# Copies of k and v between partitions in three uneven pieces, ranked setup operations and a new table of places, in a two-layer attention and mixing kernel

## The chip, the cores and the metric

The kernel runs on one core of one Trainium2 chip. The metric is the device time of one execution in microseconds. TensorE is called PE below, VectorE DVE, ScalarE ACT, GpSimd POOL, and SyncE SP. SP only issues DMAs here; ACT issues a few too.

## The reference

Two layers with the same weights, each made of two blocks, on x of 2048 positions by 512 features (fp32):

```python
x = x + A(layernorm(x));  x = x + B(layernorm(x))      # twice
# A: q, k, v = x @ wqkv, 32 heads of 16; position s looks at s, s-2, ..., s-14 (8 positions, dilation 2),
#    positions before 0 masked with -1e9; softmax over the 8; o @ wo
# B: h = gelu(layernorm(x) @ w1); its four quarters of 128 features shifted by +1, -1, +2, -2 positions; @ w2;
#    x1 = x + that;  x1 + gelu(layernorm(x1) @ w3) @ w4     (w3 is 512 x 1792)
```

## The kernel before

The 2048 positions are worked on in four blocks of 512, twice (two layers), so there are eight steps n = 0 to 7. Within a block, tile i (0 to 3) holds 128 positions: partitions 0 to 63 hold even positions and 64 to 127 odd ones ("parity"), and partition p of tile i stands for position 8p + 2i (+1) of the block. In this layout the window of dilation 2 runs along the free axis: k and v stand in buffers `kv` of 11 slots of 128 numbers, 7 of pad (the positions before) and 4 of the block's own. The pad slots of a partition are the own slots of the partition above it: slots 3 to 6 come from one partition above, slots 0 to 2 from two partitions above. There are three `kv` buffers.

For block 0 the kernel takes a short way (`p1_quarters`): q, k and v are computed in fp32 for a quarter of the heads at a time (qt 0 to 3), and the shifted pad slots are made by DMA copies between partitions of SBUF (in `p2_unit`, n = 0). Quarter 0 is written straight to `kv` buffers, quarters 1 to 3 to `x` buffers first. The copies of quarter 0 for parity 1 are issued by ACT, all others by SP. The other blocks (`p1_stream`) split fp32 numbers into two fp16 parts (tiles named `_hl`, three products for one), store q, k and v to DRAM (`q_d`, `kv_d`) through three buffers `ev`, and load the windows from there.

The attention itself (`p2_unit`) is on DVE: products of k with q over the window, sums, softmax (the exponential on ACT), products with v, a tree of sums to `o`. For each n there are four such units, one for each quarter of the heads. `p3` transposes and splits `o` to `oT` (`turn_pe`, `split`), multiplies by wo and goes on to w1; `p4` does the shifted product with w2; `p5` the MLP.

Nothing is issued in the order in which it is written. Every operation is an `Op` with a list of engines and expected durations; `Graph` finds what depends on what, and `plan` simulates the engines: at each point of simulated time, a free engine takes the ready operation with the lowest key among those for which buffers are free. The key of the k-th operation made is `PLACES[k]`, a table of ranks. What `plan` returns is issued, engine by engine, in that order; on the chip each engine works in order and waits on semaphores.

```python
o.key, o.alts, o.succ, o.n, o.est = PLACES[len(self.ops)], alts, [], 0, 0.0
...
for e in (PE, ACT, DVE, POOL, SP):
    if free[e] > now or not ready[e]:
        continue
    ...
        it = heapq.heappop(ready[e])
```

Before the first ranked operation stand setup instructions in written order: 64 warm-up products on PE, memsets of the mask, of the pad slots and of zeros, and a store of zeros to the head of `kv_d` of layer 2, issued by ACT. All ranked operations are issued through one helper, so that the profile shows them all with its line, L363; the tiles' names tell them apart.

Of the kernel before, what the change touches and what calls it, by code (L numbers as in the profile page):

```python
# [199 lines left out]


class Op:
    __slots__ = ("key", "alts", "succ", "n", "est", "touch", "seq", "fn", "end", "xfer", "eng", "lend")


class Graph:
# [3 lines left out]
    def __call__(self, key, alts, r=(), w=(), after=(), xfer=0.0):  # L210
# [34 lines left out]
        return o  # L245


LAT, LAT_PE, LAT_SP, LAT_DMA, TABLE = 0.12, 0.4, 0.3, 2.3, 1.3


def plan(ops, slots):
# [97 lines left out]
def tile_mixer(ctx, tc, x_d, wqkv_d, wo_d, w1_d, w2_d, w3_d, w4_d, out_d):  # L349
# [599 lines left out]
    def p2_unit(n, qt):  # L949
# [76 lines left out]
        for i in (0, 2):  # L1026
# [25 lines left out]
            if n == 0 and i and qt == 3:  # L1052
                o_.lend = LENT
# [316 lines left out]
```

## Time and profile before

| | |
|---|---|
| time, median of 3 runs | 1227.99 us (1225.02 to 1229.84) |
| profiled execution | 1225.26 us, of which the span of its instructions 1223.5 us |
| PE busy | 1188.0 us (97%) |
| DVE busy | 930.2 us (76%) |
| ACT busy | 629.3 us (51%) |
| POOL busy | 386.4 us (32%) |
| mean granted clock of PE | 0.992 |
| moved by DMA | 176.73 MB |

A row of a timeline has the start, the time, the engine (PEld is PE's weight load; SPq and ACTq are queues in which a DMA is issued), the line, the operation, the tiles as out<-in without buffer numbers, the shapes and how many; in brackets the idle time before and what ended it. A row of waits has who waited for whom, the microseconds in total, the times, and the longest one. A row of a table of stretches has the busy time of each engine, the granted clock of PE (1.00 is full speed), the DMA engines' mean share and GB/s.

### The profile page before, as it was taken

How to read it: one execution, taken by the hardware profiler on the slowest of the kernel's cores; microseconds unless marked ns; L12 is line 12 of the kernel's file. 1: busy time of each engine (PE TensorE's matmuls, PEld its weight loads, DVE VectorE, ACT ScalarE, POOL GpSimd, SP SyncE). 2: the span in 40 equal slices, each digit the busy share in tenths (PEclk: the TensorE clock that was granted, in tenths of full speed). 3: DMA queues.
4: the chain of work that ended last, by engine and by line, in shares of the span. 5: the costliest groups of instructions: out<-in, count | busy, mean ns of one | idle time of the engine just before them, and what ended most of it. 6: DMA issues, size and time to landing. Idle time of an engine off the chain costs nothing.

```text
span 1223.5 us, 15971 instructions
## 1 busy us (share of the span) xinstructions
PE 1188.0 (97%) x5676; PEld 589.8 (48%) x5676; DVE 930.2 (76%) x1082; ACT 629.3 (51%) x1102; POOL 386.4 (32%) x534
## 2 busy tenths in 40 slices
PE   9887889999999999999999999999999999999998
PEld 7433444555444454544454444444454444445544
DVE  4588988998889989999984899798974999414212
ACT  4543476534875345655464446555653556444422
POOL 6311265302541234314451325212632372211000
PEclk9989999999999999999999999999999999999999
DMA  5656575885676665564436543685147434111322
GB/s 172 183 161 174 148 192 168 241 233 151 191 225 173 167 169 123 132 178 116 122 90 174 159 110 110 175 201 134 59 138 214 135 91 146 61 62 48 108 77 69
DMA packets 129599, 176.73 MB, mean 144 GB/s; under 512 B 11504, under 2 KB 72912, under 8 KB 129520
## 3 DMA queue, kind: packets, MB, share of 16 engines
q1 hardware_dynamic: 127216, 173.78, 51.0%
q10 hardware_dynamic: 2304, 1.95, 0.6%
q8 instruction: 44, 0.72, 0.3%
q14 instruction: 35, 0.29, 0.1%
HBM read 132.64 MB, written 37.87 MB: 139 GB/s over the span
## 4 chain that ended last, share of the span: by engine, by line
PE 71%; DMA 0%; DVE 0%; ACT 0%; issue 0%
PE mm L363 50%; PE acc L363 21%; DMA w<-w 0%; DVE x L363 0%; ACT ev L363 0%
## 5 line engine op out<-in xcount | busy, mean ns | idle before, releaser
L363 PE MATMUL acc<-w,g 128*128 128x512 f16 (+1 forms) x1260 | 307.4, 393 | 0.2 <-DMA w<-in_B_w_dram 0.2
L363 PE MATMUL mm<-nT,w 128*128 128x512 f16 (+1 forms) x1288 | 301.5, 388 | 0.7 <-ACT nT L363 0.7
L363 PE MATMUL mm<-wq_hl,xt 128*128 128x512 f16 x1008 | 231.8, 384 | 12.0 <-ACT ev L363 9.8
L363 ACT ACTIVATE mm<-mm,s_w 128x512 f32<-128x512 f32 (+1 forms) x144 | 90.7, 630 | 207.0 <-PE mm L363 206.6
L363 PEld LDWEIGHTS <-w 128*128 128x128 f16 x1344 | 125.2, 98 | 136.9 <-DMA w<-w 0.3
L363 PEld LDWEIGHTS <-g 128*128 128x128 f16 x1176 | 114.7, 98 | 130.4 <-issue 0.3
L363 PEld LDWEIGHTS <-xt 128*128 128x128 f16 x1008 | 99.6, 99 | 128.9 <-issue 19.7
L363 DVE TENSOR_TENSOR prod<-kv,L 128x2048 f32<-128x2048 f32 x64 | 148.9, 2326 | 2.8 <-DMA kv<-kv_d 2.2
L363 DVE TENSOR_TENSOR prod<-kv,q 128x2048 f32<-128x2048 f32 x58 | 134.8, 2324 | 15.6 <-DMA kv<-kv 9.6
L363 DVE TENSOR_REDUCE L<-prod 128x128 f32<-128x2048 f32 x64 | 145.8, 2282 | 0.6
L363 DVE TENSOR_TENSOR prod<-prod 128x512 f32<-128x512 f32 (+1 forms) x129 | 131.1, 1016 | 2.5
L363 POOL TENSOR_TENSOR g<-f,g 128x512 f16<-128x512 f32 x32 | 50.7, 1587 | 235.4 <-ACT g L363 154.7
L363 PE MATMUL mm<-nT,w_hl 128*128 128x512 f16 x384 | 87.6, 379 | 0.5 <-ACT ev L363 0.3
L363 PE MATMUL mm<-wo_hl,oT 128*128 128x512 f16 x384 | 87.6, 384 | 0.0
L363 PE MATMUL mm<-w_hl,h 128*128 128x512 f16 x384 | 84.5, 379 | 0.0
L363 DVE SCALAR_TENSOR_TENSOR g<-mm,c_g,g 128x512 f16<-128x512 f32 x56 | 41.8, 746 | 51.4 <-ACT g L363 51.3
L363 ACT ACT_TABLE_LOAD x54 | 69.3, 1283 | 7.5 <-DVE mx L363 5.2
L363 ACT ACTIVATE ev<-mm,s_kv 128x512 f32<-128x512 f32 x56 | 38.3, 684 | 62.2 <-PE mm L363 55.0
L363 POOL TENSOR_SCALAR b<-b 128x1 f32<-128x1 f32 (+1 forms) x48 | 18.5, 385 | 161.6 <-ACT junk L363 159.9
L363 ACT ACTIVATE g<-mm,c_g 128x512 f16<-128x512 f32 x98 | 66.6, 685 | 1.9
L363 PEld LDWEIGHTS <-oT 128*128 128x128 f16 x426 | 42.1, 99 | 51.2 <-issue 2.8
L363 DVE TENSOR_TENSOR nT<-mm,nT 128x512 f16<-128x512 f32 x60 | 40.9, 688 | 33.4 <-ACT nT L363 32.7
(189 smaller groups left out, 1438.7 us busy)
## 6 DMA issues: line engine op xcount, KB each, us to landing
w<-w SPq DMA_DIRECT2D x196, 256.0 KB
kv<-kv_d SPq DMA_DIRECT2D x112, 352.0 KB
w<-in_B_w_dram SPq DMA_DIRECT2D x56, 256.0 KB
kv_d<-ev SPq DMA_DIRECT2D x112, 128.0 KB
q_d<-ev SPq DMA_DIRECT2D x28, 256.0 KB
q<-q_d SPq DMA_DIRECT2D x28, 256.0 KB
w<-g SPq DMA_DIRECT2D x28, 256.0 KB
x<-x SPq DMA_DIRECT2D x27, 256.0 KB
```

Of the source, the lines that this page charges most:

```text
L363: i = f(*a, **k).ins
```

## The change

Three things are changed together. The copies between partitions of block 0 ran from parity to parity: for each of k and v, and for each quarter, four copies of 63 rows (4 slots) and 62 rows (3 slots), two for each parity. Now they take both parities at once: 126 rows of 3 slots, shifted by two partitions, and 4 slots shifted by one partition in 112 and 15 rows. The rows that cross from parity 0 into the first partitions of parity 1 land where the mask stands. For quarter 0 the copy of 112 rows is issued by ACT. Second, the memsets of mask and pad (the latter now for the head of parity 0 only) and the zeros of `kv_d` become ranked operations, the zeros as two DMAs on SP from an `ev` buffer; 40 warm-up products stand for 64. Third, `plan` is given other durations, other first free times of the engines and a model of 8 DMA lanes, and the table of places is new throughout: 3153 ranks for 3157.

```diff
-    __slots__ = (..., "eng", "lend")
+    __slots__ = (..., "eng", "lend", "parts")
...
 LAT, LAT_PE, LAT_SP, LAT_DMA, TABLE = 0.12, 0.4, 0.3, 2.3, 1.3
+FREE = (7.0, 1.0, 1.5, 1.0, 1.1)
+LANES = 8
...
-    free = [0.0] * 5
+    free = list(FREE)
+    lane, lanes = 0, [0.0] * LANES
...
             if o.xfer:
-                free[e] = now + d
-                dma_free = max(dma_free, now + d) + o.xfer
+                begin = max(now, *(lanes[(lane + k) % LANES] for k in range(o.parts)))
+                free[e] = begin + d
+                dma_free = max(dma_free, begin + d) + o.xfer
                 o.end = dma_free + LAT_DMA
+                for k in range(o.parts):
+                    lanes[lane] = o.end
+                    lane = (lane + 1) % LANES
...
-    WARM = 64
+    WARM = 40
...
-    G.memset(maskb, 0.0)
-    for base in (0, 64):
-        ...
-    zero = slots["prod"][0][:16, :PAD * P]
-    V.memset(zero, 0.0)
...
-    A.dma_start(at(kv_d[1], [[RS, 16], [1, PAD * P]]), zero)
-    for j in range(len(slots["kv"])):
-        for base in (0, 64):
-            G.memset(slots["kv"][j][base:base + 1, 3 * P:PAD * P], 0.0)
-            G.memset(slots["kv"][j][base:base + 2, :3 * P], 0.0)
...
+    def set_mask():
+        G.memset(maskb, 0.0)
+        ...
+    def set_pad():
+        for j in range(len(slots["kv"])):
+            G.memset(slots["kv"][j][:1, 3 * P:PAD * P], 0.0)
+            G.memset(slots["kv"][j][:2, :3 * P], 0.0)
+    gp(-5.0, 3.0, set_pad, [], [pad[0]])
+    gp(-5.0, 3.0, set_mask, [], [mask_b])
+    zero = Buf("ev")
+    dve(-4.0, 0.3, lambda: V.memset(zero.t[:16], 0.0), [], [zero])
+    zeros = op(-4.0, [(SP, 0.9, lambda: [Y.dma_start(at(kv_d[1][0, 0, 0, k], [[RS, 16], [1, n * P]]), zero.t[:16, :n * P])
+                                 for k, n in ((0, 4), (4, 3))], None)], [zero], [pad[1]], xfer=0.1)
+    zeros.parts = 2
...
-                for par in range(2):
-                    for d, s0, n_ in ((1, 3, NT), (2, 0, 3)):
-                        dma(k1 + 0.01, ..., kv[j].t[64 * par + d:64 * par + 64, s0 * P:(s0 + n_) * P],
-                            ..., src[j].t[64 * par:64 * par + 64 - d, first + (NT - n_) * P:first + NT * P],
-                            [(src[j], tiles)], [(kv[j], ("sh", par, d))], 0.4, by_act=qt == 0 and par == 1)
+                for m, (d, s0, n_, p0, p1) in enumerate(((2, 0, 3, 0, P - 2), (1, 3, NT, 0, 112),
+                                                         (1, 3, NT, 112, P - 1))):
+                    sh_op = dma(k1 + 0.01, ..., kv[j].t[p0 + d:p1 + d, s0 * P:(s0 + n_) * P],
+                        ..., src[j].t[p0:p1, first + (NT - n_) * P:first + NT * P],
+                        [(src[j], tiles)], [(kv[j], ("sh", m))], (0.8, 0.8, 0.1)[m], by_act=qt == 0 and m == 1)
...
-                    ..., [kv[j]], 1.9,
+                    ... + [pad[1]] * (n == NB), [kv[j]], 2.6,
...
-                    [P, 2, W, P]), ALU.mult), q_in + kv_in[0], [pr, (L, "new")], lock=True)
+                    [P, 2, W, P]), ALU.mult), q_in + kv_in[0] + [pad[0]] * (n == 0), [pr, (L, "new")], lock=True)
...
-        dve(kd, 0.85 + (0.45 if b == 0 else 0), soft, [], [mx, all_L], lock=True)
+        dve(kd, 0.88 + (0.45 if b == 0 else 0), soft, [mask_b] * (b == 0), [mx, all_L], lock=True)
...
-    TREE = [3] + [3] * 7
-        tree, by_pe = TREE[n], TREE[n] < 3
...
```

Where only an expected duration was changed, the line is left out here: there are some fifteen of them, such as 0.6 to 0.9 for a power on POOL and 0.32 to 0.28 for one evacuation of block 0 on ACT. The branch with `TREE` and `by_pe` (sums of the tree on PE) goes away with its code.

More of the change, by code (lines that the diff above doesn't have):

```diff
@@ L202 @@
 class Op:
-    __slots__ = ("key", "alts", "succ", "n", "est", "touch", "seq", "fn", "end", "xfer", "eng", "lend")
+    __slots__ = ("key", "alts", "succ", "n", "est", "touch", "seq", "fn", "end", "xfer", "eng", "lend", "parts")
 class Graph:
@@ L214, in __call__ @@
         o.key, o.alts, o.succ, o.n, o.est = PLACES[len(self.ops)], alts, [], 0, 0.0
-        o.seq, o.xfer, o.lend = len(self.ops), xfer, ()
+        o.seq, o.xfer, o.lend, o.parts = len(self.ops), xfer, (), 1
         before, touch = set(after), {}
@@ L450, in tile_mixer @@
     maskb = const.tile([P, NT, W], F32, name="maskb")
-    G.memset(maskb, 0.0)
-    for base in (0, 64):
-        for i in range(NT):
-            if i < 3:
-                G.memset(maskb[base:base + 2, i, 0:3 - i], -1e9)
-            G.memset(maskb[base:base + 1, i, 0:7 - i], -1e9)
     ident = const.tile([P, P], F32, name="ident")
@@ L492, in fn @@
                 Y.dma_start(out(par), in_(par))
-        return op(key, [(SP, 1.15, fn, None)], r, w, after, xfer)
+        o = op(key, [(SP, 1.15, fn, None)], r, w, after, xfer)
+        o.parts = 2
+        return o
     def par_of(t, par):
@@ L510, in tile_mixer @@
     GELU, EXP = "gelu", "exp"
+    op.stage = ("first", None)
+    mask_b, pad = Buf(), [Buf(), Buf()]
+    def set_mask():
+        G.memset(maskb, 0.0)
+        for base in (0, 64):
+            for i in range(NT):
+                if i < 3:
+                    G.memset(maskb[base:base + 2, i, 0:3 - i], -1e9)
+                G.memset(maskb[base:base + 1, i, 0:7 - i], -1e9)
+    def set_pad():
[9 more added lines that the diff above has]
+    zeros.parts = 2
     xd1 = [dram.tile([P, NT, D], F32, name=f"x1_{b}") for b in range(NB)]
@@ L552, in bound @@
             V.tensor_scalar(f2.t[:, :m], v, 1e-30, 1e30, ALU.max, ALU.min)
-        dve(key, 0.35, bound, [ps], [f2])
+        dve(key, 0.2, bound, [ps], [f2])
         p = inv.t[:, :m] if inv.kind is None and not isinstance(inv.t, tuple) else inv.t
-        gp(key, 0.6, lambda: G.tensor_tensor(p, f2.t[:, :m], nhalf[:, :m], ALU.pow), [f2], [inv])
+        gp(key, 0.9, lambda: G.tensor_tensor(p, f2.t[:, :m], nhalf[:, :m], ALU.pow), [f2], [inv])
         def cut():
@@ L639, in fn @@
             G.tensor_scalar(nb.t[:, s], tot.t[:, k:k + 1], r.t[:, s], c, ALU.mult, ALU.mult)
-        gp(key, 1.0, fn, [(ss, j), (tot, k)], [(ve, i), (r, i), (nb, i)])
+        gp(key, 1.2, fn, [(ss, j), (tot, k)], [(ve, i), (r, i), (nb, i)])
     C0 = -1.0 / D
@@ L704, in p1_norm @@
         if l == 0 and b >= STATS:
-            act(key, 0.85, lambda: A.activation(junk, src(), AF.Identity, accum_out=tot.t[:, i:i + 1]),
+            act(key, 0.64, lambda: A.activation(junk, src(), AF.Identity, accum_out=tot.t[:, i:i + 1]),
                 [x], [(tot, i)])
@@ L766, in out @@
                                          scale=1.0 if k else DH ** -0.5)
-                    done = act(key, 0.32 * len(ks), out, [ps], [(d, i) for d in dst])
+                    done = act(key, 0.1 + 0.18 * len(ks), out, [ps], [(d, i) for d in dst])
                     if qt == 0 and i == NT - 1 and ks[0] == 0:
@@ L854, in small_weight @@
         hl = wt.t.rearrange("p (a f) -> p a f", a=2)
-        act(key, 2.1, lambda: A.activation(hl[:, 0].bitcast(BF16), v(), AF.Square, accum_out=ss.t),
+        act(key, 1.92, lambda: A.activation(hl[:, 0].bitcast(BF16), v(), AF.Square, accum_out=ss.t),
             [(st, list(range(NC)))], [wt, ss])
@@ L882, in big_pair @@
                 dma(key - 0.5, v, lambda i=i: w4_d[P * i:P * (i + 1), :], [], [t], 0.8, begun)
-            act(key, 0.72, lambda v=v, m=m: A.activation(
+            act(key, 0.64, lambda v=v, m=m: A.activation(
                 junk, v(), AF.Square, accum_out=ss_p[c].t[:, m:m + 1]), [t], [(ss_p[c], m)])
@@ L960, in p2_unit @@
             q_in = [(q, list(range(NT)))]
-            sh = [("sh", par, d) for par in range(2) for d in (1, 2)]
+            sh = [("sh", k) for k in range(3)]
             kv_in = [[(k, [("own", 0), *sh] if qt else list(range(NT)) + sh)] for k in kv]
@@ L969, in p2_unit @@
                                         [(src[j], tiles)], [(kv[j], ("own", 0)), (kv[j], "new")], 0.8)
-                for par in range(2):
-                    for d, s0, n_ in ((1, 3, NT), (2, 0, 3)):
-                        dma(k1 + 0.01, lambda j=j, par=par, d=d, s0=s0, n_=n_, kv=kv: kv[j].t[
-                                64 * par + d:64 * par + 64, s0 * P:(s0 + n_) * P],
-                            lambda j=j, par=par, d=d, n_=n_, src=src, first=first: src[j].t[
-                                64 * par:64 * par + 64 - d, first + (NT - n_) * P:first + NT * P],
-                            [(src[j], tiles)], [(kv[j], ("sh", par, d))], 0.4, by_act=qt == 0 and par == 1)
+                for m, (d, s0, n_, p0, p1) in enumerate(((2, 0, 3, 0, P - 2), (1, 3, NT, 0, 112),
+                                                         (1, 3, NT, 112, P - 1))):
+                    sh_op = dma(k1 + 0.01, lambda j=j, d=d, s0=s0, n_=n_, p0=p0, p1=p1, kv=kv: kv[j].t[
+                                p0 + d:p1 + d, s0 * P:(s0 + n_) * P],
+                        lambda j=j, n_=n_, p0=p0, p1=p1, src=src, first=first: src[j].t[
+                            p0:p1, first + (NT - n_) * P:first + NT * P],
+                        [(src[j], tiles)], [(kv[j], ("sh", m))], (0.8, 0.8, 0.1)[m], by_act=qt == 0 and m == 1)
+                    if not qt:
+                        first_q.setdefault("shifted", []).append(sh_op)
         else:
@@ L985, in p2_unit @@
                     kv_d[l][j, qt, p, 256 * b], [[NT * P, 64], [1, NSL * P]]),
-                    [(kvb[l], [(*c, j) for c in cells + prev])], [kv[j]], 1.9,
+                    [(kvb[l], [(*c, j) for c in cells + prev])] + [pad[1]] * (n == NB), [kv[j]], 2.6,
                     [first_q["copied"]] if n < 3 else ())
@@ L1018, in norm @@
             V.tensor_mul(L4(), L4(), wide(sm))
-        dve(kd, 1.22, norm, [], [sm, all_L], lock=True)
+        dve(kd, 1.27, norm, [], [sm, all_L], lock=True)
         oT = Buf("oT")
@@ L1023, in p2_unit @@
         hl = lambda a: oT.t.rearrange("p (k a f) -> a p k f", a=2, k=NT)[a]
-        tree, by_pe = TREE[n], TREE[n] < 3
-        ps = Buf("mm") if by_pe else None
         for i in (0, 2):
@@ L1032, in p2_unit @@
                 Lv()[:, i:i + 2].unsqueeze(4).to_broadcast([P, 2, W, H8, DH]), ALU.mult),
-                [all_L, *kv_in[1]], [pr] if by_pe else [pr, (o, 9)], lock=True)
+                [all_L, *kv_in[1]], [pr, (o, 9)], lock=True)
             def add(i=i, pv4=pv4, ov=ov):
-                p, m = pv4(), W
-                for k in range(tree):
-                    m //= 2
-                    V.tensor_add(ov()[:, i:i + 2] if m == 1 else p[:, :, 0:m],
-                                 p[:, :, 0:m] if m > 1 else p[:, :, 0], p[:, :, m:2 * m] if m > 1 else p[:, :, 1])
-            if tree:
-                o_ = dve(kd + 0.01, (0, 1.22, 1.92, 2.45)[tree], add, [], [pr] if by_pe else [pr, (o, i)], lock=True)
-            if by_pe:
-                def turn_sum(i=i, pv4=pv4):
-                    m = W >> tree
-                    for t in range(2):
-                        f = slice(P * (i + t), P * (i + t) + P)
-                        for j in range(m):
-                            T.matmul(ps.t[:, f], pv4()[:, t, j], ident, start=(i + t + j == 0),
-                                     stop=(i + t + j == NT + m - 2))
-                o_ = pe(ko, 2 * (W >> tree) * 0.2 + 0.1, turn_sum, [pr], [ps, (oT, "new")])
-            if n == 0 and i and qt == 3:
-                o_.lend = LENT
-        if by_pe:
-            split(ko, ps, oT, [0], lambda: hl(0), lambda: hl(1), c_o)
-            return oT
+                p = pv4()
+                V.tensor_add(p[:, :, 0:4], p[:, :, 0:4], p[:, :, 4:8])
+                V.tensor_add(p[:, :, 0:2], p[:, :, 0:2], p[:, :, 2:4])
+                V.tensor_add(ov()[:, i:i + 2], p[:, :, 0], p[:, :, 1])
+            added = dve(kd + 0.01, 2.45, add, [], [pr, (o, i)], lock=True)
+        if n == 0 and qt == 3:
+            added.lend = LENT
         turn_pe(ko, o, oT, [0], lambda: hl(0), lambda: hl(1), [(o, [0, 2])], scale=c_o)
@@ L1111, in p3 @@
         tiles = list(range(NT))
-        gp(key + 0.2, 1.8, r1_of, [(ss, tiles), (sums, tiles)], [(r1, tiles), ve1, (nb1, tiles)])
+        gp(key + 0.2, 2.3, r1_of, [(ss, tiles), (sums, tiles)], [(r1, tiles), ve1, (nb1, tiles)])
         h = hs[n] = Buf("h")
@@ L1142, in p3 @@
                 e = slice(8, 9 + (g == 2))
-                gp(key, 0.4, lambda g=g, k=k, e=e: G.tensor_copy(
+                gp(key, 0.49, lambda g=g, k=k, e=e: G.tensor_copy(
                     hview(h)[:, :, g, k, 1:64], hview(h)[:, :, g, e, 0:63]), own, [(h, ("L", g))])
@@ L1154, in p3 @@
                 e = slice(0, 1 + (g == 3))
-                gp(key, 0.4, lambda g=g, k=k, e=e: G.tensor_copy(
+                gp(key, 0.49, lambda g=g, k=k, e=e: G.tensor_copy(
                     hview(h)[:, :, g, k, 0:63], hview(h)[:, :, g, e, 1:64]), own, [(h, ("R", g))])
@@ L1225, in p4 @@
                 turn_pe(key + 0.01 * k, nr, dst, [k], lambda cols=cols: cols(0), lambda cols=cols: cols(1), [nr])
-            op(key + 0.3, [(POOL, 1.2, lambda src=src, x1=x1: G.tensor_add(src(), src(), x1.t), None),
+            op(key + 0.3, [(POOL, 1.25, lambda src=src, x1=x1: G.tensor_add(src(), src(), x1.t), None),
                            (DVE, 0.72, lambda src=src, x1=x1: V.tensor_add(src(), src(), x1.t), "lock")],
@@ L1246, in plain_chunk @@
         pe(key, NC * K * 0.214, up, [w3, (nT, [(k, 0) for k in range(K)])], [ps, (g, "new")])
-        act(key, 0.2 + 0.115 * K, lambda: A.activation(f32v(g.t, D)[:, :P * K], ps.t[:, :P * K],
+        act(key, 0.15 + 0.115 * K, lambda: A.activation(f32v(g.t, D)[:, :P * K], ps.t[:, :P * K],
                                                        AF.Gelu_apprx_tanh, scale=1.0 / SN), [ps], [g], cls=GELU)
```

264 rows, old and new, of the table PLACES are left out of this document.

## The prediction

> **What bounds the kernel now.** I read the page first, then a table of stretches, then the timelines of VectorE and TensorE in the stretch that the table pointed at.
>
> ```profile
> span 1223.5 us, 15971 instructions
> PE 1188.0 (97%) x5676; PEld 589.8 (48%) x5676; DVE 930.2 (76%) x1082; ACT 629.3 (51%) x1102; POOL 386.4 (32%) x534
> PE 71%; DMA 0%; DVE 0%; ACT 0%; issue 0%
> ```
>
> TensorE (PE) is busy for 1188.0 of 1223.5 us, so 35.5 us of the span are not PE work, and that is most of what a change of order can win. The chain says the same: it is PE wherever it can be followed. The next table tells where the 35.5 us lie (columns: stretch, its length, busy time of PE, PEld, DVE, ACT, POOL with counts, granted clock, DMA share, GB/s).
>
> ```profile
> 0.00:40.00 40.00, 38.06 (x198) 28.46 (x198) 19.58 (x35) 17.97 (x46) 23.04 (x56) 1.00 0.64 181
> 40.00:60.00 20.00, 14.90 (x45) 8.06 (x43) 12.53 (x14) 12.94 (x42) 8.81 (x15) 0.93 0.60 166
> 60.00:80.00 20.00, 19.99 (x85) 9.26 (x83) 16.44 (x14) 11.98 (x30) 5.60 (x10) 0.98 0.58 169
> 80.00:100.00 20.00, 15.20 (x64) 7.09 (x65) 18.06 (x18) 7.31 (x15) 2.21 (x5) 0.83 0.63 168
> 100.00:120.00 20.00, 13.87 (x62) 6.58 (x61) 16.58 (x19) 6.60 (x13) 2.56 (x3) 0.91 0.68 175
> 120.00:140.00 20.00, 17.90 (x87) 8.43 (x85) 15.24 (x14) 7.49 (x14) 0.00 (x0) 1.00 0.70 178
> 140.00:160.00 20.00, 16.00 (x71) 7.29 (x70) 17.88 (x29) 10.16 (x19) 11.54 (x8) 0.91 0.56 145
> 160.00:240.00 80.00, 76.02 (x351) 38.03 (x349) 71.50 (x93) 53.26 (x101) 41.44 (x58) 1.00 0.68 193
> 240.00:360.00 120.00, 117.16 (x456) 59.97 (x455) 106.27 (x139) 67.78 (x123) 37.27 (x55) 1.00 0.72 204
> 360.00:1200.00 840.00, 839.95 (x4158) 407.12 (x4157) 630.81 (x705) 430.32 (x696) 253.97 (x327) 1.00 0.46 129
> ```
>
> From 360 to 1200 us PE has no hole: nothing can be won there, and the new table can only lose. Between 40 and 160 us PE idles 5.10+0.01+4.80+6.13+2.10+4.00 = 22.0 us, and the clock granted is short by 0.07+0.02+0.17+0.09+0.00+0.09 = 0.44 of a 20 us slice, 8.8 us. In 160 to 240 us it idles 4.0 us, in 240 to 360 us 2.8 us. So the stage to read is 40 to 160 us: the attention of block 0 on VectorE (DVE), beside the projections of blocks 1 and 2 on PE. What ends the holes there is seen on DVE (last bracket: idle before, and what ended it):
>
> ```profile
> 34.34 0.61 DVE L363 SCALAR_TENSOR_TENSOR wq_hl<-nT,inv_q,wq_hl 128x384 f16<-128x384 f32 x1
> 44.51 2.29 DVE L363 TENSOR_TENSOR prod<-kv,q 128x2048 f32<-128x2048 f32 x1 [9.56 <-DMA kv<-kv]
> ...
> 63.42 2.29 DVE L363 TENSOR_TENSOR prod<-kv,x 128x2048 f32<-128x2048 f32 x1 [4.11 <-DMA kv<-x]
> ...
> 124.62 0.75 DVE L363 SCALAR_TENSOR_TENSOR oT<-mm,c_o,oT 128x512 f16<-128x512 f32 x1 [5.29 <-ACT oT L363]
> ...
> 153.88 0.43 DVE L363 TENSOR_TENSOR o<-prod 128x256 f32<-128x256 f32 x1
> ```
>
> ```profile
> 156.31 3.96 PE L363 MATMUL mm<-wo_hl,oT 128*128 128x512 f16 x10
> ```
>
> DVE has split the weights of q, k and v at 34.95 us and then stands still for 9.56 us, until a copy of k between partitions has landed; a second copy holds it for 4.11 us; the last attention sum of block 0 ends at 154.31 us, and 2.0 us later PE starts the output projection of block 0. Everything of block 0 after that (the mixing, then the MLP) hangs on this DVE chain, so a microsecond won on it is a microsecond of the end as long as PE can be filled.
>
> **The change, part by part.** *The copies.* They are what DVE waits for:
>
> ```profile
> kv<-kv SPq DMA_DIRECT2D x1, 93.0 KB
> ```
>
> ```profile
> 38.45 0.69 SPq L363 DMA_DIRECT2D kv<-kv  x1
> ```
>
> ```profile
> SPq L363 <- DMA kv<-x: 6.7, 6, 2.0
> SPq L363 <- DMA kv<-kv: 6.2, 4, 3.1
> ```
>
> ```profile
> L363 SPq DMA_DIRECT2D kv<-x x30: 515/698/1337, 50.4 to 114.9; - x30
> ```
>
> The copy issued at 38.45 us has 93.0 KB, that is 62 rows of 1536 bytes (slots 0 to 2, shifted by two partitions); DVE goes on at 44.51, 6.06 us after the issue. The DMA queue of SP itself stood still 6.7 + 6.2 = 12.9 us behind such copies before 160 us, with loads and stores of other blocks queued behind. The change makes 3 copies of 126, 112 and 15 rows out of 4 of 62, 63, 62 and 63, for k and v of each quarter: 24 issues for 32. Eight issues at 0.698 us are 5.6 us of queue time less, off the path by themselves. The first price to bound is how long a new copy takes. From above: 6.06 us, like the old one. From below: an unhindered load has done it in about 3.3 us (two issues of 64 rows from 0.72 us on, with the first statistic released at 4.24):
>
> ```profile
> 0.72 2.50 SPq L363 DMA_DIRECT2D w<-in_A_x_dram  x4
> ```
>
> ```profile
> 4.24 0.69 DVE L363 BATCH_NORM_STATS2 mx<-w 128x6 f32<-128x512 f32 x1 [2.32 <-DMA w<-in_A_x_dram]
> ```
>
> I take a value near the lower end, since no row shows the new shapes at work but the queue ahead of them is shorter. [...]
>
> *Their places.* The table gives each operation its rank in the order it is made. In the old table quarter 0's k copies had 149 and 186 on SP, 150 and 155 on ACT, and loads of x and of w3 and w4 with 161, 168, 179, 180 went ahead of the 186. In the new one they have 176 and 177 on SP and 119 on ACT, and apart from block 0's own x and wqkv only one load, of w3 (147), stands ahead. So k of quarter 0 is sent as soon as it is evacuated, which is over by 24.63 us:
>
> ```profile
> 24.35 0.28 ACT L363 ACTIVATE kv<-mm 128x128 f32<-128x128 f32 x1 [0.31 <-PE mm L363]
> ```
>
> With two SP issues of 0.7 us behind it and even 6.06 us to land, the copies are in by 32.1 us, before DVE is free at 34.95. The 9.56 us go whole. Next late is DVE's own weight split, which is work. The 4.11 us for quarter 1 are less sure. In the new ranks quarter 0's products with v (239 and 250) go before quarter 1's first (268), which gives the second set of copies some 9 us of cover, two products at 2.29 us with their sums; but quarter 1's copies (232 to 253, one of v 290) have stores and loads among them. From both sides: nothing, or 4.11 us; I take half, 2.1 us. The 5.29 us at 124.62 come from ACT, which is late itself: nothing to 5.29 us, and I take nothing, as no row ties it to the copies.
>
> *Setup as ranked operations, and 40 warm-up matmuls for 64.* These rows show the start:
>
> ```profile
> 2.83 5.45 POOL L363 MEMSET kv<- 1x512 f32 x12
> 8.37 0.19 POOL L363 TENSOR_SCALAR a<-mx 128x1 f32<-128x1 f32 x1
> ```
>
> ```profile
> 1.95 0.37 ACTq L363 DMA_DIRECT2D kv_d<-prod  x1
> 2.35 2.79 ACTq L363 DMA_DIRECT2D nT<-in_A_wqkv_dram  x4
> ```
>
> ```profile
> 1.03 9.57 PE L363 MATMUL mm<-ones 128*128 128x256 f16 x64 [1.03 <-DVE ones L363]
> ...
> 12.03 1.13 PE L363 MATMUL mm<-nT,g 128*128 128x256 f32 x4 [0.91 <-ACT g L363]
> ```
>
> The memsets of kv halve (12 to 6, 2.7 us of POOL), the mask's stay, and the first statistic on POOL, at 8.37 us right behind them, may come 2.7 us sooner. ACT's first weight load waits at 2.35 us behind the store of zeros, which moves to SP, as two issues among the x and weight loads. SP's first issue is at 0.72, so ACT's could be 1.6 us earlier. The first product at 12.03 needs both; the bounds are 0 and 1.6 us, and I take 0.8, since SP now carries the zeros. The 24 warm-up matmuls taken away are 24 × 9.57/64 = 3.6 us of PE, hidden while PE waits for its first tile. The new waits of block 0's first attention operations for mask and pad hide behind the 34.95 us before DVE needs them; the one for the zeros in DRAM is asked for by layer 2 alone, hundreds of microseconds later. The memset of zeros on DVE is not on the path either.
>
> *The rest.* The changed durations, first free times and DMA lanes only enter the ordering program; they run nothing. Removing the branch with TREE changes no instruction: TREE held 3 everywhere. What the new order does to 160 to 1200 us no row of before can show. Its bounds are the 6.8 us of holes in 160 to 360 us as a gain, and, as a loss, one more wait like the largest seen, 9.56 us; nearest is the row with 839.95 of 840, and I take nothing.
>
> Sum against the profiled execution: 1225.26 us (span 1223.5, 1.8 around it) − 9.56 − 2.1 − 0.8 = 1212.8, so 1213. PE can take it up: 12.5 us are 57% of its 22.0 us of holes in that stage. The median of the runs, 1227.99, stands 2.7 us above the profiled one, which I keep inside the range.
>
> **The rivals.** *PE's own queue holds the gain back.* In the first 160 us PE waits not for DVE but for ACT, which empties its accumulators and stands behind loads:
>
> ```profile
> ACT junk L363 <- DMA w<-in_B_w_dram: 18.9, 4, 6.1
> PE mm L363 <- ACT ev L363: 12.0, 10, 4.3
> ```
>
> If these 12.0 us stay and are not shortened by DVE's earlier start, only 22.0 − 12.0 = 10.0 us of holes can close, and of DVE's 12.5 perhaps half is seen: 1225.3 − 6 = 1219. For it: the 12.0 and 18.9 us. Against: those loads share the queue in which the old copies cost 12.9 us, and DVE's chain, not ACT's, ends at the output projection.
>
> *Everything closes.* With the copies short, the stores that free PE's evacuation buffers land sooner too: 1.6 + 9.56 + 4.11 + 5.29 and the 4.0 us of 160 to 240 are 24.6 us, 1201. Against: every hole would have to be a DMA's.
>
> *The copies stay slow*, because contention and not their shape made them so: 6.06 us each again, the waits move to the next quarter, and only the start's 0 to 1.6 us remain: 1225.
>
> *Slower: a head-of-line wait in quarter 3.* Its first products rank 73 and 99 on DVE, so the ordering program puts them in as soon as it thinks their copies are in, and the copies stand at 390 to 440 in SP's order among the stores of blocks 1 and 2. DVE works in order: if SP is late, the splits that feed PE stand behind the wait. One such wait at the price of the row above (9.56 us) eats most of the 12.5 us; from 18.6 us on, two of them, the kernel is over 0.5% slower, 1232. For it: SP's 12.9 us of standing. Against: the smaller number of copies.
>
> *A cold start.* Forty warm-ups end at 1.03 + 9.57 × 40/64 = 7.0 us, and a hole up to the first transposes could cost clock as the holes of 40 to 60 us did (0.07 of 20 us, 1.4 us): 1214, inside the forecast. [...]
>
> **How the numbers follow.** Half a per cent (6.1 us around 1227.99, so under 1221.9 or over 1234.1) is about what this kernel's measurement can tell from no change. Chances: the forecast, 1205 to 1217, 0.48; everything closes, under 1205, 0.16; PE's queue holds it back, 1217 to 1222, 0.15; copies stay slow or are paid back, 1222 to 1234, 0.14; slower, 0.07. Faster is 0.48 + 0.16 + 0.15 = 0.79. The range 1199 to 1223 leaves out about 0.05 below and 0.15 above.
>
> **What the profile after would show.** Right: DVE's first product with kv at 33 to 36 us, not held by a kv copy; no DMA row named kv for SP's waits above 2 us in all; the first statistic on POOL before 6 us; the output projection of block 0 on PE at 142 to 146 us; PE idle between 40 and 160 us near 10 us and the clock above 0.95 there; the stretch after 360 us still without holes. Wrong: a wait of DVE for kv of 5 us or more later on; new holes of PE behind 360 us; or PE idle by ACT as before while DVE runs early.

## The result

The kernel after takes 1206.05 us (median, 1204.81 to 1206.34) against 1226.51 us (1224.72 to 1229.84) before in the same rounds: ratio 0.983, interval 0.980 to 0.985. Run again beside the experiments below it took 1204.78 us, ratio 0.982 (0.980 to 0.984). The forecast was 1213 with 1199 to 1223 around it: the sign and the range hold, and the gain, 20.5 us, is 8 us more than the sum of 12.5. The profiled execution took 1204.81 us, as against 1225.26 before.

The page of the kernel after, its head and the busy time of the engines:

```profile
span 1203.0 us, 15906 instructions
PE 1178.4 (98%) x5652; PEld 586.9 (49%) x5652; DVE 926.1 (77%) x1082; ACT 639.6 (53%) x1118; POOL 355.9 (30%) x512
```

The same table of stretches as in the prediction, for the kernel after (stretch, length, busy time of PE, PEld, DVE, ACT, POOL with counts, granted clock, DMA share, GB/s):

```profile
0.00:40.00 40.00, 36.12 (x173) 26.17 (x174) 22.47 (x36) 25.35 (x63) 14.37 (x45) 1.00 0.80 217
40.00:60.00 20.00, 19.26 (x75) 10.48 (x74) 15.87 (x15) 15.70 (x48) 8.47 (x19) 1.00 0.56 174
60.00:80.00 20.00, 18.45 (x91) 9.69 (x90) 19.30 (x26) 11.62 (x22) 6.83 (x7) 1.00 0.79 214
80.00:100.00 20.00, 17.36 (x88) 8.60 (x86) 19.16 (x23) 12.17 (x25) 6.37 (x8) 1.00 0.79 216
100.00:120.00 20.00, 18.11 (x82) 8.47 (x80) 18.51 (x18) 8.45 (x16) 1.70 (x2) 0.91 0.79 198
120.00:140.00 20.00, 19.29 (x96) 9.47 (x94) 18.88 (x33) 11.07 (x19) 3.71 (x4) 1.00 0.71 176
140.00:160.00 20.00, 18.50 (x95) 9.21 (x93) 16.10 (x28) 18.41 (x43) 11.99 (x25) 1.00 0.72 226
160.00:240.00 80.00, 78.00 (x305) 40.10 (x304) 73.45 (x73) 37.75 (x58) 21.77 (x24) 0.98 0.62 168
...
360.00:1200.00 840.00, 835.23 (x4158) 405.88 (x4156) 613.69 (x693) 421.83 (x688) 241.36 (x321) 1.00 0.45 126
```

The 20.5 us of span come from two columns. PE's idle time falls from 35.5 to 1203.0 − 1178.4 = 24.6 us, which is 10.9 us; PE's busy time falls from 1188.0 to 1178.4, which is 9.6 us for the same 5612 products (5652 with the warm-ups, of which there are 24 fewer). Where the idle time went: between 40 and 160 us it is 0.74 + 1.55 + 2.64 + 1.89 + 0.71 + 1.50 = 9.0 us, for 22.0 before. In the first 40 us it grew from 1.9 to 3.9, with fewer warm-ups to cover it, and behind 360 us there is a little more of it. Where the busy time went: 2.9 us are the warm-ups (9.57 to 6.63 us), and most of the rest is the clock, whose shortfall was 8.8 us between 40 and 160 us, and is in the stretches up to 240 us now 0.09 × 20 + 0.02 × 80 = 3.4 us. So in these two executions products were slower where the clock was lower: `mm<-wq_hl,xt` of 128x512 took 432 ns at the mean between 80 and 100 us before (0.83), 406 ns between 100 and 120 us after (0.91), and 379 ns between 120 and 140 us in both (1.00). Five of the six stretches from 40 to 160 us were short of clock before, one after. That the holes made the clock lower is not shown; the last section has more runs on it.

VectorE and TensorE of the kernel after, the rows that answer to those of the prediction:

```profile
33.75 2.27 DVE L370 TENSOR_TENSOR prod<-kv,q 128x2048 f32<-128x2048 f32 x1
...
48.76 2.29 DVE L370 TENSOR_TENSOR prod<-kv,x 128x2048 f32<-128x2048 f32 x1 [1.42 <-DMA kv<-x]
```

```profile
1.03 6.63 PE L370 MATMUL mm<-ones 128*128 128x256 f16 x40 [1.03 <-DVE ones L370]
...
10.98 1.99 PE L370 MATMUL mm<-nT,g 128*128 128x256 f32 x8 [1.00 <-ACT g L370]
...
133.86 5.34 PE L370 MATMUL mm<-wo_hl,oT 128*128 128x512 f16 x24
```

DVE's first product with k starts at 33.75 for 44.51 and waits for nothing; the second set waits 1.42 us for 4.11; the output projection of block 0 starts on PE at 133.86 for 156.31, 22.5 us earlier. What held SP's queue up to 160 us, and what held PE and ACT in the same stretch (waiter, releaser, microseconds in total, times, longest):

```profile
SPq L370 <- ACT ev L370: 13.1, 10, 2.2
SPq L370 <- ACT kv L370: 10.4, 1, 10.4
...
SPq L370 <- DMA kv<-kv: 0.2, 1, 0.2
```

```profile
PE mm L370 <- ACT ev L370: 6.0, 7, 1.5
ACT junk L370 <- DMA w<-in_A_x_dram: 5.5, 6, 1.9
...
ACT junk L370 <- DMA w<-in_B_w_dram: 1.0, 1, 1.0
```

Of the copies, 12.9 us in that list before, 0.2 us is left. SP now waits above all for producers, and still 10.6 us for other transfers, 7.8 before. And the waits that the prediction took as a rival fell too: PE behind ACT's evacuations from 12.0 to 6.0 us, ACT's statistics (`junk`) behind loads of the weights of B (`in_B_w_dram`) from 18.9 to 1.0, and behind loads of x from 15.8 to 5.5.

### The profile page after: what moved, and what is told of

Same layout as the page of the kernel before. It is cut to its first block, busy times and chain, and to the rows that moved or that the text cites. A ratio compares the mean times of both kernels' runs of the same rounds, so it can differ in the third digit from the quotient of the medians.

```text
span 1203.0 us, 15906 instructions
## 1 busy us (share of the span) xinstructions
PE 1178.4 (98%) x5652; PEld 586.9 (49%) x5652; DVE 926.1 (77%) x1082; ACT 639.6 (53%) x1118; POOL 355.9 (30%) x512
## 4 chain that ended last, share of the span: by engine, by line
PE 90%; DMA 3%; ACT 3%; POOL 1%; DVE 1%; issue 1%; SPq 1%; ACTq 0%; POOLq 0%; DVEq 0%
PE mm L370 67%; PE acc L370 24%; DMA w<-in_A_x_dram 1%; ACT junk L370 1%; SPq L370 1%; DMA h<-in_A_wqkv_dram 1%; DMA x<-in_A_x_dram 0%; DMA nT<-in_A_wqkv_dram 0%; ACT ev L370 0%; ACT f L370 0%; POOL c L370 0%; POOL x L370 0%; DMA w<-in_B_w_dram 0%; POOL b L370 0%; ACT xt L370 0%
## 5 line engine op out<-in xcount | busy, mean ns | idle before, releaser
L370 PE MATMUL mm<-nT,w 128*128 128x512 f16 (+1 forms) x1288 | 304.6, 390 | 0.9 <-ACT nT L370 0.9
L370 PE MATMUL mm<-wq_hl,xt 128*128 128x512 f16 x1008 | 226.7, 381 | 3.8 <-ACT ev L370 3.8
L370 DVE TENSOR_TENSOR prod<-prod 128x1024 f32<-128x1024 f32 (+1 forms) x129 | 134.4, 1042 | 2.7
L370 POOL TENSOR_TENSOR g<-f,g 128x512 f16<-128x512 f32 x32 | 46.4, 1452 | 172.6 <-ACT f L370 103.2
L370 POOL COPY h<-h 128x126 f16<-128x126 f16 (+3 forms) x56 | 42.8, 786 | 81.7 <-DVE h L370 79.7
```

Of the source, the lines that this page charges most:

```text
L370: i = f(*a, **k).ins
```

## The experiments

The theory is the prediction's: the gain is the 9.56 us for which DVE stood at its first product with k, and half of the next such wait (the first wait, below). Its rivals: the copies are short now, but what counts is what stands behind them in SP's queue; or the gain is the new table's; or it is the start's.

**The copies alone.** The kernel before with the new row ranges; the fourth copy of each set stays in the order as an operation that issues nothing, so that the old table, durations and setup hold, and the order of the work is the old one.

```diff
+ p0, p1 = {(0, 1): (112, P - 1), (0, 2): (0, P - 2), (1, 1): (0, 112), (1, 2): (0, 0)}[par, d]
+ if p1:
-     dma(..., kv[j].t[64 * par + d:64 * par + 64, ...], src[j].t[64 * par:64 * par + 64 - d, ...], ...)
+     dma(..., kv[j].t[p0 + d:p1 + d, ...], src[j].t[p0:p1, ...], ...)
+ else:
+     op(k1 + 0.01, [(ACT or SP, ..., lambda: None, None)], ...)
```

> The kernel before, with its old table, durations and setup, and only the copies of block 0 in the new shapes (126, 112 and 15 rows; the fourth operation of each set issues nothing). Shape theory: the copies of 62 rows held DVE, SP's queue and the stores behind them, so most of the gain is here: about 1211 to 1215 us, DVE's first product at about 35 to 37 us instead of 44.5, and no wait of SP for kv copies over 1 us. Order theory: the old table sends the last k copy of quarter 0 as late as 38.45 us whatever its shape, so DVE starts at about 41.5 us and the time falls by 3 us or less, to 1223 us.

Measured: 1208.81 us, ratio 0.985 (0.984 to 0.987). So about 18 of the 20.5 us are the copies' and need no new table. Shape and number go together here: this kernel also issues 8 DMAs fewer. The time is a little below what the first of the two expectations had, and DVE's start is what the second had. Since every engine issues the old order, the two traces can be laid side by side row by row. DVE of this kernel:

```profile
41.23 2.29 DVE L363 TENSOR_TENSOR prod<-kv,q 128x2048 f32<-128x2048 f32 x1 [7.65 <-DMA kv<-kv]
...
54.64 1.17 DVE L363 SCALAR_TENSOR_TENSOR wo_hl<-nT,inv_wo,wo_hl 128x512 f16<-128x512 f32 x1 [1.88 <-POOL wo_hl L363]
55.73 2.28 DVE L363 TENSOR_TENSOR prod<-kv,x 128x2048 f32<-128x2048 f32 x1
...
107.39 0.75 DVE L363 SCALAR_TENSOR_TENSOR oT<-mm,c_o,oT 128x512 f16<-128x512 f32 x1
```

DVE still waits 7.65 us for k, since the copy of k is still sent late, and is not quick either (SP issues its 126 rows at 35.98, and DVE starts 5.25 us later):

```profile
35.98 0.85 SPq L363 DMA_DIRECT2D kv<-kv  x1
```

And yet nearly the whole gain is there. That already speaks against the first wait as the source. The lead over the kernel before grows later: at the second set of products it is 63.42 − 55.73 = 7.7 us, at the `oT` of 107.39 it is 124.62 − 107.39 = 17.2. The same group of instructions has these rows in the kernel before, from SP to DVE:

```profile
46.48 2.23 SPq L363 DMA_DIRECT2D w<-in_A_x_dram  x2
```

```profile
54.25 0.63 ACT L363 ACTIVATE junk<-w 128x512 bf16<-128x512 f32 x1 [6.79 <-DMA w<-in_A_x_dram]
```

```profile
57.42 3.13 POOL L363 TENSOR_SCALAR wo_hl<-nT,inv_wo 128x512 f16<-128x512 f32 x4
```

```profile
58.15 1.17 DVE L363 SCALAR_TENSOR_TENSOR wo_hl<-nT,inv_wo,wo_hl 128x512 f16<-128x512 f32 x1 [2.10 <-POOL wo_hl L363]
```

and these with the copies alone:

```profile
43.23 1.13 SPq L363 DMA_DIRECT2D w<-in_A_x_dram  x2
```

```profile
50.75 0.63 ACT L363 ACTIVATE junk<-w 128x512 bf16<-128x512 f32 x1 [4.98 <-DMA w<-in_A_x_dram]
```

```profile
53.91 5.24 POOL L363 TENSOR_SCALAR wo_hl<-nT,inv_wo 128x512 f16<-128x512 f32 x4
```

Read them from the top: SP issues two loads of x, behind the copies of quarter 0; ACT's statistic waits for them, POOL's scale waits for ACT, POOL's first part of the weight split of wo stands behind that on POOL, and DVE's second part, in order ahead of the second set of products, waits for POOL. Load to DVE takes 11.67 us before and 11.41 us here, and the load is issued 3.25 us earlier (between 24 and 50 us SP stands 0.5 us behind copies, 4.9 before): DVE is 3.5 us ahead at that place. The wait of 4.11 us for the second copies is gone: 7.6 of the 7.7 us. From there to 106.03 in the kernel before (94.00 here) the lead grows by 4.3 us, of which 2.47 us are a wait of DVE for ACT's `oT`; and by 5.2 us more up to 124.62 (107.39 here), where another such wait of 5.29 us stood. DVE's rows for the first of these, before and with the copies alone:

```profile
106.03 0.75 DVE L363 SCALAR_TENSOR_TENSOR oT<-mm,c_o,oT 128x512 f16<-128x512 f32 x1 [2.47 <-ACT oT L363]
```

```profile
94.00 0.74 DVE L363 SCALAR_TENSOR_TENSOR oT<-mm,c_o,oT 128x512 f16<-128x512 f32 x1
```

ACT was late in the kernel before because it stood behind stores that had to give back an `ev` buffer, and behind loads:

```profile
101.34 0.69 ACT L363 ACTIVATE ev<-mm,s_kv 128x512 f32<-128x512 f32 x1 [2.12 <-DMA kv_d<-ev]
...
112.63 0.63 ACT L363 ACTIVATE junk<-w 128x512 bf16<-128x512 f32 x1 [6.15 <-DMA w<-in_B_w_dram]
```

With the copies alone the first of these waits is gone, and the statistic of the second waits 4.88 us less, in the stretch in which the lead grows by 5.2:

```profile
95.45 0.63 ACT L363 ACTIVATE junk<-w 128x512 bf16<-128x512 f32 x1 [1.27 <-DMA w<-in_B_w_dram]
```

At the output projection 15.7 us of the lead are left, and of the span 16.7 us:

```profile
140.59 12.52 PE L363 MATMUL mm<-wo_hl,oT 128*128 128x512 f16 x48
```

**Copies of 62 rows again, with a control.** In the kernel after, the copy of 126 rows is cut in three, once into 62 + 2 + 62 rows and once into 48 + 48 + 30, the same number of DMAs and of bytes.

```diff
-    q_.dma_start(kv[j].t[p0 + d:p1 + d, ...], src[j].t[p0:p1, ...])
+    for a, b_ in (((0, 62), (62, 64), (64, 126)) if d == 2 else ((p0, p1),)):   # control: (0, 48), (48, 96), (96, 126)
+        q_.dma_start(kv[j].t[a + d:b_ + d, ...], src[j].t[a:b_, ...])
```

> The changed kernel in its new order, each copy of 126 rows issued as three DMAs of 62, 2 and 62 rows. Same bytes and same number of issues as the run with 48, 48 and 30 rows. [...] Order theory: the new order sends the copies early enough, so the two differ by under 3 us.

> The control to the run with 62, 2 and 62 rows: the same three issues for the copy of 126 rows, as 48, 48 and 30 rows. 16 issues more than the changed kernel at about 0.6 us are 10 us of SP's queue; both theories expect 0 to 4 us over the changed kernel's 1206 us.

Measured: 1223.56 us (ratio 0.997, 0.996 to 0.999) with 62 rows, 1213.16 us (0.989, 0.986 to 0.992) with the control. What SP waited for among the copies up to 160 us, with 62 rows (the control has no such rows):

```profile
SPq L370 <- DMA kv<-kv: 4.2, 4, 2.2
SPq L370 <- DMA kv<-x: 3.3, 4, 1.1
```

ACT's statistics of x behind their loads and DVE's first wait for a copy, with 62 rows:

```profile
ACT junk L370 <- DMA w<-in_A_x_dram: 21.0, 7, 4.5
```

```profile
57.89 2.29 DVE L370 TENSOR_TENSOR prod<-kv,x 128x2048 f32<-128x2048 f32 x1 [5.16 <-DMA kv<-x]
```

and in the control:

```profile
ACT junk L370 <- DMA w<-in_A_x_dram: 14.4, 7, 3.9
```

```profile
51.90 2.29 DVE L370 TENSOR_TENSOR prod<-kv,x 128x2048 f32<-128x2048 f32 x1 [4.59 <-DMA kv<-x]
```

The row count alone is worth 10.4 us, with the new order, the same bytes and the same number of issues. The waits are the old ones: SP stands 7.5 us behind copies, ACT 6.6 us longer behind loads, and DVE's second set is 6.0 us later though its own wait for the copy is only 0.6 us longer. Why 62 rows are slower, no row of these runs shows. The control itself is 7 us slower than the kernel after, which sends the 126 rows in one copy; that is more than I expected. Its ACT stands 14.4 us behind loads of x, for 5.5 there. The author's guess at the reason is the 16 more DMAs on SP (the issues of `kv<-x` took 594 ns at the median there, 36 of them, for 24 at 806 ns in the kernel after); no run shows that by itself. If 16 more cost 7 us, the 8 fewer of the copies-alone kernel may be some 3 of its 18 us (an estimate).

**The first wait alone.** The copies-alone kernel, and quarter 0's k in 126 rows is issued along with the 15 rows, at the first of SP's copies; nothing else changes its place on any queue.

```diff
+ if qt == 0 and j == 0 and par == 0:      # k of quarter 0: both pieces at the first copy's place
+     op(k1 + 0.01, [(SP, 0.45, both if d == 1 else lambda: None, None)], [(src[j], tiles)], [(kv[j], ("sh", par, d))], (), 0.4)
```

> The kernel before with the new copies, and the 126 rows of quarter 0's k issued together with the 15 rows, at SP's first copy; nothing else moves on any queue (the run with the changed rank had another order from end to end, so it told nothing of this wait). Theory of the prediction (DVE's first wait is on the path): DVE's first product at about 35 us instead of 41.2, and the time 5 to 7 us under the 1208.8 us of the new copies alone, 1202 to 1204 us. Rival (the wait is made up later): within 2 us of 1208.8 us, with the output projection of block 0 no more than 2 us before 140.6 us.

Measured: 1209.13 us, ratio 0.985 (0.983 to 0.987); it stood at 0.985 with the wait. DVE of this kernel:

```profile
33.89 2.28 DVE L363 TENSOR_TENSOR prod<-kv,q 128x2048 f32<-128x2048 f32 x1
...
45.87 0.16 DVE L363 TENSOR_SCALAR mx<-mm 128x1 f32<-128x1 f32 x1 [5.18 <-PE mm L363]
...
55.40 1.17 DVE L363 SCALAR_TENSOR_TENSOR wo_hl<-nT,inv_wo,wo_hl 128x512 f16<-128x512 f32 x1 [3.49 <-POOL wo_hl L363]
```

then two of ACT's statistics of x, the first ahead of the row at 45.87 and the second ahead of that at 55.40, and SP's issue of the second one's loads:

```profile
39.58 0.63 ACT L363 ACTIVATE junk<-w 128x512 bf16<-128x512 f32 x1 [5.28 <-DMA w<-in_A_x_dram]
...
51.50 0.63 ACT L363 ACTIVATE junk<-w 128x512 bf16<-128x512 f32 x1 [3.91 <-DMA w<-in_A_x_dram]
```

```profile
44.27 1.13 SPq L363 DMA_DIRECT2D w<-in_A_x_dram  x2
```

The wait of 7.65 us is gone and DVE is 7.3 us ahead at 33.89. Then it waits 5.18 us for PE and 3.49 us for POOL, each of which comes after an ACT that waits for loads of x, and at 55.40 it is 0.8 us behind the run without this edit. The load was issued 1.04 us later than there, and from load to DVE it is 11.1 us. The output projection starts at 141.43, for 140.59. So the theory falls: taking away the 7.65 us that were left of the prediction's main wait gains nothing that can be measured, for 5 to 7 us that it should have gained, and by these rows the issue of the load on SP sets when the second set of products starts.

Two limits of this. The copy that was moved ahead put the load back by 1.04 us, so the run does not show the move with the loads where they were; by the rows above, with the load at 43.23, DVE would have come to its place at 54.64 no sooner. And with the copies alone k lands 3.28 us sooner than in the kernel before (41.23 for 44.51). Had it not, the same rows would have brought DVE there at 56.04 (44.51, and the 11.53 us from 41.23 to its being free for that row at 52.76), so up to 1.4 of the 3.5 us do hang on k.

I first tried the same by one rank in the table of the copies-alone kernel.

```diff
+PLACES[347] = 148.5      # was 186: the copy of k that lands last
```

> The run with the new copies in the kernel before, with one rank more changed: the last k copy of quarter 0 (126 rows) from 186 to 148.5, ahead of the loads of x and w that SP issued before it. There DVE still waited 7.7 us for it (first product at 41.2 us). Theory of the prediction (DVE's first wait is on the path that sets the end): first product at about 35 us and 5 to 7 us less than that run, 1202 to 1204 us. Rival (what the new shapes win comes from later, from SP's queue and the stores behind it, and a wait of DVE at 35 us is made up by 140 us): first product at 35 us, but the time within 2 us of that run's 1208.8 us.

Measured: 1237.25 us, ratio 1.007 (1.006 to 1.009). DVE's first product started at 29.4 us, so the copy was early; but the order written out by the simulated engines differed from there to the end, and PE lost 8.3 us between 160 and 240 us and 10.1 us between 240 and 360. It tells nothing of the wait, and much of the table: one rank in 3157 cost 28 us. Neither expectation had that.

**The table and its durations.** The kernel after with the old table's ranks (setup operations first, each new copy at an old one's rank); with the new table but the old durations, first free times and no lanes; and with the old of both.

```diff
 PLACES = [...]            # old ranks:  those of the table before
-FREE = (7.0, 1.0, 1.5, 1.0, 1.1)
+FREE = (0.0, 0.0, 0.0, 0.0, 0.0)          # old durations: this, begin = now, and the old times
```

> The changed kernel with its copies, ranked setup and new durations, but every operation that both kernels have at its rank of the old table (setup first, each new copy at the rank of an old one). Shape theory: within 4 us of the changed kernel, 1205 to 1210 us. Order theory: the new table is worth most of the 20.5 us, so 1217 to 1225 us.

> The changed kernel with its new table, but durations, first free times and lanes of the ordering program as before. If the table and the durations only work together (the run with the old ranks under the new durations took 1236 us), this one is slower than the changed kernel by 8 us or more, 1214 to 1235 us. If the old ranks lost for a reason of their own, it stays within 4 us of 1206 us.

> The changed kernel's copies and ranked setup with the old ranks and the old durations, first free times and no lanes. If ranks and durations only work together, this one is back near the run with the new copies alone, 1205 to 1212 us, 24 us or more under the old ranks with the new durations (1236 us). If the setup operations or the ranks by themselves were to blame, it stays above 1225 us.

Measured: old ranks 1236.04 us (ratio 1.007, 1.005 to 1.009), old durations 1230.50 us (1.002, 1.000 to 1.003), both old 1234.10 us (1.006, 1.003 to 1.008). The first lies outside both of its expectations, the second inside its first one. With the old durations the output projection starts at 133.90 us, as in the kernel after, and then this stands in PE's timeline and in the table of stretches:

```profile
217.02 2.82 PE L370 MATMUL mm<-ident,f 128*128 128x128 f32 x12 [13.34 <-ACT f L370]
```

```profile
160.00:240.00 80.00, 64.37 (x269) 32.80 (x270) 75.97 (x74) 33.83 (x54) 23.57 (x26) 0.91 0.57 153
```

One hole of 13.34 us and a clock of 0.91 in its stretch (0.09 × 80 = 7.2 us) pay back what the copies won. With both old I had expected the gain back, on the idea that ranks and durations only fit together; it did not come. Two sets of ranks and durations fit this work, the old with its old list of operations, and the new with its own; each of the four mixtures that were tried (the one rank among them) came out at 1230 to 1237 us. So the table is a rival in part only: it brings little over the new copies in the old order (1206.05 and 1204.78 us against 1208.81, and 1209.13 with the first wait taken away; the ratio intervals overlap), but in these tries no table and durations that were not made together for a list of operations held the gain.

**The start.** The kernel after with mask, all 12 pad memsets and the zeros' store in written order ahead of everything, their ranked operations empty; and the kernel after with 64 warm-ups.

```diff
-    gp(-5.0, 3.0, set_pad, [], [pad[0]]); gp(-5.0, 3.0, set_mask, [], [mask_b])
+    G.memset(maskb, 0.0); ...; V.memset(zero0, 0.0); A.dma_start(at(kv_d[1], ...), zero0); G.memset(kv ..., 0.0)   # as before
```

> The changed kernel with mask, all 12 pad memsets and the store of zeros in front in written order, as before; the ranked operations for them issue nothing. The prediction's term for the start (0.8 us, between 0 and 1.6): 1206 to 1208 us, with the first product on PE 0 to 1.6 us later than the 10.98 us of the changed kernel. Rival (the load of the start is limited by DMA, not by POOL or by ACT's queue): no change within 0.5 us.

```diff
-    WARM = 40
+    WARM = 64
```

> The changed kernel with 64 warm-up products for 40. They would end at about 10.6 us, after the first transpose's start at 9.33 us in the changed kernel, so 0 to 1.5 us slower, 1206 to 1207.5 us. Were a cold start the price of 40, this one would be up to 2 us faster.

Measured: setup in front 1212.05 us (ratio 0.986, 0.984 to 0.988), 64 warm-ups 1207.18 us (0.982, 0.981 to 0.984). With the setup in front PE's first product starts at 12.18 us for 10.98, 1.2 us later, within what was expected; the time is 3.5 us longer by the profiled executions and 6 by the medians. That is outside the 1206 to 1208 us expected, and what makes more of it than the 1.2 us was not settled. With 64 warm-ups the first product starts 0.6 us later and the time is the same within its interval, so the start is a matter of some 1 to 6 us, and the number of warm-ups of none that can be measured.

**Copies alone, first wait and start together**, to see whether the old table can reach the new one's time: the first-wait kernel with 40 warm-ups, half the pad memsets and ACT's zeros behind its first weight load.

```diff
-    WARM = 64
+    WARM = 40
-    A.dma_start(at(kv_d[1], ...), zero)        # now behind ACT's load c == 0
```

> The same, with the start of the changed kernel but in written order: 40 warm-up products, half the pad memsets, the store of zeros on ACT behind its weight loads. The prediction's 0.8 us for the start (0 to 1.6): 0 to 1.6 us under the run before. By the run with the setup in front of the changed kernel (6 us slower) more could be seen, up to 4 us.

> The changed kernel on the same chip, for comparison: 1204 to 1207 us.

Measured: 1207.41 us (1204.36 to 1209.87), ratio 0.984 (0.981 to 0.986), beside the kernel after at 1204.78 us on the same chip, 0.982 (0.980 to 0.984), and 1.7 us under the first-wait kernel (0.985, 0.983 to 0.987). All three intervals overlap; no kernel here is clearly better than the kernel after, and what the new table adds to the copies and the start is not told from nothing.

## Why the prediction was right, and where it was not

*The sign, the range and the place.* The idle time of PE between 40 and 160 us was named as what there was to win, with the copies as the cause and some 10 us of idle time left; 9.0 are left. The clock came to 1.00 in every slice of that stretch but one (0.91 from 100 to 120 us). The output projection came 8 us sooner than the earliest time forecast, at 133.86 for 142 to 146 us: the forecast was short of the gain there too.

*New copies are quick.* The row count mattered: the 62-row run and its control, with the same bytes and the same number of issues, are 10.4 us apart. The rival in which the copies stay slow and only the start is won (1225 us) is out. The size, "near the lower end" of 3.3 to 6.06 us, is not borne out: the one time that can be read plainly for a copy of 126 rows, with a reader waiting for it alone, is the 5.25 us with the copies alone, nearer the upper end, for twice the bytes of the old copy. The 3.3 us were read low, too: from the issue at 0.72 us to the statistic at 4.24 are 3.52.

*"The 9.56 us go whole."* This is the step that failed. They did go: DVE's first product starts at 33.75 us, inside the 33 to 36 of the prediction. But they were not on the path. Taking away what the new shape had left of the same wait, 7.65 us, moved nothing, because behind it DVE waits for PE and POOL, who hang on loads of x. The working asked what DVE does once it is released (its own splits and products), and not whether the operations behind, in DVE's order, have their other inputs by then. The rows for it were at hand in the trace of before: the wait of 2.10 us for POOL at 58.15, 14 us behind the freed one, followed back to the load at 46.48.

*"Half of 4.11."* Undersized: with the copies alone it went whole, and in the kernel after 1.42 us of a like wait are left.

*"5.29 us at 124.62: I take nothing, as no row ties it to the copies."* With the copies alone it is gone, in the old order. What tied it were ACT's waits for loads and stores in the same queue; the prediction quoted ACT's 18.9 and SP's 12.9 us and took no term of its sum from them. With the 2.47 us at 106.03 and the 3.5 us of the load's chain, these later terms carry the gain that the main term was credited with: 3.5 + 4.1 + 4.3 + 5.2 = 17.1 us up to 124.62.

*The clock.* It had no term in the sum though its 8.8 us were worked out; some 5 of them are gone in the profiled execution after.

*"PE's own queue holds the gain back"* named the right link, PE behind ACT, with the wrong sign: that wait shrank by half, from 12.0 to 6.0 (to 4.4 with the copies alone, in the old order). The loads that ACT waits for share the queue that the copies held up (by the 12.9 us), which the prediction had put down as the argument against. *"Everything closes"* had the mechanism (stores and loads land sooner), but not every hole is a DMA's: 24.6 us of idle time are left.

*The start.* 0.8 us was taken; the first product came 1.05 us sooner. But the first statistic on POOL, which was to be ahead of 6 us, came at 7.23 (8.37 before), since its load lands later (DVE waits for it until 6.14 us, for 4.24 before); from POOL's and DVE's timelines of the kernel after:

```profile
7.23 0.19 POOL L370 TENSOR_SCALAR a<-mx 128x1 f32<-128x1 f32 x1 [1.90 <-DVE mx L370]
```

```profile
6.14 0.69 DVE L370 BATCH_NORM_STATS2 mx<-w 128x6 f32<-128x512 f32 x1 [4.62 <-DMA w<-in_A_x_dram]
```

DVE's first statistic is 1.9 us later than before, though SP issues its loads of x from 0.71 us on, as before (0.72). ACT's weight loads are now issued beside them, from 0.72 us on for 2.35; whether they are what holds up the load of x was not tried by itself. Having half the memsets won POOL 3.0 us (the last one of `kv` ends at 5.33 us for 8.28) and lost most of it to the later load: POOL then waits 1.90 us for DVE.

*"Behind 360 us still without holes"* was wrong by a small sum. There are two, from PE's timeline of the kernel after:

```profile
429.37 0.66 PE L370 MATMUL mm<-ident,f 128*128 128x128 f32 x4 [2.04 <-ACT f L370]
430.72 2.61 PE L370 MATMUL mm<-nT,w_hl 128*128 128x512 f16 x10 [0.69 <-ACT nT L370]
```

*The slower rival*, a wait in quarter 3, did not come in this table. The runs with mixed ranks and durations show that the danger it stood for is real, and its price: 13.34 us in one hole.

So the number came near in part by luck, as two errors met: a main term of 9.56 us of which no more than some 1.4 can be seen in the lead, and later terms of some 17 us, and the clock, that were put at 2.1.

## What to carry to other kernels

A wait is worth what is left when its end moves, so walk on from the freed instruction along its engine's order and look at the next waits for other engines: if one of them ends by a load that does not move along, the gain ends there too. Here the slow copies cost most through what was queued behind them (of the 17.1 us won up to 124.62, at most 1.4 hang on the first wait for k and 4.1 were the wait for the second copies); when the shape of a copy is mended, look for the gain at the loads and stores behind it and at whoever waits for those, rather than at its own reader. To test one wait, move its DMA and nothing else: a rank in a table that drives a greedy planner moves the whole program (here one in 3157 cost 28 us).

## What the runs showed of the hardware

At the same bytes, the row counts of the copies between partitions mattered: in the same order, 62 + 2 + 62 rows took the kernel 10.4 us longer than 48 + 48 + 30. Cutting them finer cost time too: in three pieces of 48, 48 and 30 rows, 16 DMAs more, the kernel was 7 us slower than with 126 in one.

The clock did not simply follow the sum of PE's holes. Between 40 and 160 us the kernel before had 22.0 us of holes and fell short by 8.8 us, the run with 62 rows 19.4 and 7.0, the copies alone 12.8 and 3.6, the kernel after 9.0 and 1.8. But the run with the old ranks had 15.9 us of holes there, and the one with the old durations 12.9, and both show 1.00 in all six slices. What sets it was not tested.
